# Rebuilding the opening of a fused attention and FFN kernel: 1 KB loads, two-bank score tiles, mixing per head pair, an FFN that begins per k-tile

## The chip, the cores and the metric

The kernel runs on one core of one Trainium2 chip. The metric is the device time in microseconds (us) of one execution. Each execution also has a span (first to last instruction of its trace) and a mean granted TensorE clock; in nearly every run here the time is the span plus 1.7 us.

Executions are compared when they are of the same state: "fast" within 1.5% of the fastest of the same kernel, "slow" above that. A ratio is the mean time of one kernel's fast runs over the mean of the other's in the same rounds, so it is not quite the ratio of the medians quoted beside it. Each call of runs shares one chip and its own runs of the kernel before.

Names: PE is TensorE's matmuls, PEld its weight loads, DVE is VectorE, ACT ScalarE, POOL GpSimd, SP SyncE. L442 is line 442 of the kernel profiled; the same statement has another line number in another kernel.

## The reference, cut to what matters

```python
# 8 batches, 8 heads, 576 positions, head size 64; float32 in and out
scores = q @ k.T / 8 + min(bias, 0), causal mask        # bias from a cumulative sum of s
x = softmax(scores) @ v                                 # heads joined: (8, 576, 512)
u = x + (x.T @ U @ V).T                                 # low rank mixing over positions, rank 32
out = u + relu(u @ w_ch1) @ w_ch2                       # FFN 512 -> 2048 -> 512
```

The FFN is most of the work. It runs in nine groups of 512 rows over the flattened batches. Group 0 lies wholly in batch 0; so no FFN work exists until batch 0 has been through attention and mixing. Everything before that is called the opening here.

## The kernel before: the parts that matter

```python
ps_s = tile_pool(name="ps_s", bufs=4, space=PSUM)   # score tiles, one bank each, 512 columns
ps_w = tile_pool(name="ps_w", bufs=4, space=PSUM)   # everything else
...
# loads, all on one software DMA queue, issued by POOL in this order:
load_qk(0, 0, 2); load_qk(0, 2, 2)       # q and k of batch 0, heads 0-3
...                                      # a memset that the next one waits for
load_qk(0, 4, 4)                         # heads 4-7
load_v(0)                                # v of batch 0: one 256 B row per head and position
U, V, w1, w2
load_qk(1, 0, H); load_v(1)              # batch 1
load(2)                                  # q, k, v of batch 2
...
def spin(n, ps):                         # dummy matmuls that keep TensorE's clock up
...
def scores(n, spins=0):                  # one head pair; 7 exponentials, at most 512 columns
    tail = pscore()
    for hh in range(2):
        diag = pscore()
        ...                              # 4 matmuls
        nc.scalar.activation(pT[:, hh, 0:512], diag, EXP, scale=scale)
        ...                              # mask by a min on DVE
        far = pscore(); ...; mid = pscore(); ...
...
# the opening
for n in range(PB):                      # PB = 4 head pairs of batch 0
    drain(scores(n, 1))
    if n + 2 < PB: drain(transposes(n + 2))
    if n > 0: drain(values(n - 1))
drain(values(PB - 1))
spin(4, pscore)
for _ in seqmix(0):                      # mixing of batch 0, all four pairs together
    spin(2, pscore)
load(2)
fill.append(chanmix(0))                  # FFN of group 0
pace[1] = 8
fill_with(14)                            # 14 of its 16 hidden groups of 4 matmuls
pace[1] = 3                              # from here 3 of 8 calls of step_fill do FFN work
run(transposes(PB))                      # batch 1 begins: needs its q and k
for n in range(PB, NP + 2):              # attention of batches 1-7, FFN steps dealt in between
    ...                                  # pace[1] becomes 7 once batch 1 is mixed
```

In the traces PE runs its matmuls in the program's order. When one stands (sits idle) for a load, the FFN steps behind it are held back, too.

The softmax here doesn't subtract the row's maximum and nothing guards it: scores larger than these inputs give would overflow.

Of the kernel before, what the change touches and what calls it, by code (L numbers as in the profile page):

```python
# [39 lines left out]
def kernel(  # L40
# [12 lines left out]
    nc = tc.nc  # L53
# [21 lines left out]
    ps_s = ctx.enter_context(tc.tile_pool(name="ps_s", bufs=4, space=bass.MemoryType.PSUM))  # L75
    ps_w = ctx.enter_context(tc.tile_pool(name="ps_w", bufs=4, space=bass.MemoryType.PSUM))

    def pscore():
        return ps_s.tile([128, 512], FP32, tag="s", name="pscore")
# [9 lines left out]
    nc.sync.dma_start(out=s_sb, in_=s.rearrange("b h s -> (b h) s"))  # L89

# [6 lines left out]
    def load_qk(b, h, n):  # L97
# [5 lines left out]

    alloc_qk(0)
# [3 lines left out]
    load_qk(0, 2, 2)  # L108

    keep = consts.tile([128, 1, 128], BF16)  # L110
    nc.gpsimd.memset(keep, 3.0e38)
    nc.gpsimd.affine_select(
        out=keep,
        in_=keep,
        compare_op=ALU.is_ge,
        fill=0.0,
        base=0,
        pattern=[[0, 1], [1, 128]],
        channel_multiplier=-1,
    )  # L120


    PW = 1664
    pTs = [consts.tile([128, 2, PW], BF16, name=f"pT{i}") for i in range(2)]

    def ones(ap):
        nc.vector.memset(ap.bitcast(mybir.dt.uint32), 0x3F803F80)

    busy = consts.tile([128, 512], BF16)
    ones(busy)  # L130
# [17 lines left out]
    def spin(n, ps):  # L148
        for _ in range(n):
            dst = ps()  # L150
            nc.tensor.matmul(  # L151
                dst, lhsT=busy[:, 0:128], rhs=busy[:, 0 : dst.shape[1]], start=True, stop=True
            )
# [17 lines left out]
    for dst in (q_t[0], k_t[0]):  # L171
        nc.vector.memset(dst[:, 4:8, 0:2], 0.0)
    load_qk(0, 4, 4)
    init_v(nc.vector, v_slots[0])
    for pT in pTs:
        nc.vector.memset(pT[:, :, 1600:], 1.0)
    U_sb = consts.tile([128, 5, R], BF16)
    nc.vector.memset(U_sb[64:, 4, :], 0.0)

    V_sb = consts.tile([128, 4, S], BF16)  # L180
    nc.vector.memset(V_sb, 0.0)
# [6 lines left out]
    def load_v(b):  # L188
        vt = v_slots[b % 3]
        if 0 < b < 3:  # L190
            init_v(nc.gpsimd, vt)
        for t in range(4):
            nc.gpsimd.dma_start(  # L193
                out=vt[:, t, :, 0:D],
                in_=v[b, :, ds(t * 128, 128), :].rearrange("h p d -> p h d"),
            )
        nc.gpsimd.dma_start(
            out=vt[:64, 4, :, 0:D], in_=v[b, :, 512:576, :].rearrange("h p d -> p h d")
        )

    load_v(0)
    w1_sb = consts.tile([128, 4, FF], BF16)
    w2_sb = consts.tile([128, NF, DM], BF16)
    nc.gpsimd.dma_start(
        out=U_sb[:, :4, :], in_=moe_U[:512].rearrange("(kt kp) r -> kp kt r", kp=128)
    )
    nc.gpsimd.dma_start(out=U_sb[:64, 4, :], in_=moe_U[512:576])
    nc.gpsimd.dma_start(out=V_sb[:R, 0, :], in_=moe_V)
    nc.gpsimd.dma_start(out=w1_sb, in_=moe_w_ch1.rearrange("(kt kp) n -> kp kt n", kp=128))
# [3 lines left out]
    load_v(1)  # L213
# [8 lines left out]


    def transposes(n):
        b, hp = divmod(n, PB)
        slot = slots[n % NSLOT]
        if b > 0:
            nc.sync.dma_start(
                out=slot[D:KA, :, 0 : 2 * S],
                in_=rows_hbm[:, ds(2 * n, 2)].rearrange("r n c s -> r n (c s)"),  # L230
            )
        for hh in range(2):
            h = 2 * hp + hh
            tp = pwork().bitcast(BF16)[:, : 2 * 4 * TP].rearrange(
                "p (c t m) -> p c t m", c=2, t=4
            )
            for c, src in enumerate((q_t[b], k_t[b])):
                for t2 in range(4):
                    nc.tensor.transpose(  # L239
                        tp[:, c, t2, :], src[:, h, ds(t2 * 128, 128)], identity[:TP, :TP]  # L240
                    )
            dst = slot[0:D, hh, 0 : 2 * S].rearrange("p (c m t two) -> p c m t two", c=2, t=4, two=2)
            for par in range(2):
                copy = nc.scalar.copy if n == 0 or (b == 1 and par) else nc.vector.tensor_copy
                copy(  # L245
                    dst[:, :, :, :, par],
                    tp[par * D : par * D + D].rearrange("p c t m -> p c m t"),
                )
            yield

    def scores(n, spins=0):
        slot = slots[n % NSLOT]
        pT = pTs[n % 2]
        tail = pscore()
        for hh in range(2):
            qT = slot[0:KA, hh, 0:S]
            kT = slot[0:KA, hh, S:]

            def mm(dst, j, lo, hi):
                nc.tensor.matmul(  # L260
                    dst,
                    lhsT=kT[:, ds(j * 128, 128)],
                    rhs=qT[:, lo:hi],
                    start=True,
                    stop=True,
                )

            diag = pscore()
            for j in range(4):
                mm(diag[:, ds(j * 128, 128)], j, j * 128, j * 128 + 128)  # L270
            nc.scalar.activation(pT[:, hh, 0:512], diag, EXP, scale=scale)  # L271
            nc.vector.tensor_tensor(  # L272
                pT[:, hh, 0:512].rearrange("p (a b) -> p a b", a=4),
                pT[:, hh, 0:512].rearrange("p (a b) -> p a b", a=4),
                keep.to_broadcast([128, 4, 128]),
                op=ALU.min,
            )
            mm(tail[:, ds(hh * 64, 64)], 4, 512, S)
            spin(spins, lambda: tail[:, 128:512])
            yield  # L280
            far = pscore()
            mm(far[:, 0:448], 0, 128, S)
            mm(far[:, 448:512], 3, 512, S)
            nc.scalar.activation(pT[:, hh, 512:1024], far, EXP, scale=scale)  # L284
            mid = pscore()
            mm(mid[:, 0:320], 1, 256, S)
            mm(mid[:, 320:512], 2, 384, S)
            nc.scalar.activation(pT[:, hh, 1024:1536], mid, EXP, scale=scale)
            spin(spins if hh == 0 else 0, lambda: tail[:, 128:512])
            if hh == 1:  # L290
                nc.scalar.activation(
                    pT[:, :, 1536:1600],
                    tail[:, 0:128].rearrange("p (a b) -> p a b", a=2),
                    EXP,
                    scale=scale,
                )
                nc.vector.tensor_tensor(  # L297
                    pT[:, :, 1536:1600],
                    pT[:, :, 1536:1600],
                    keep[:, :, 0:64].to_broadcast([128, 2, 64]),  # L300
                    op=ALU.min,
                )
            yield
# [7 lines left out]
    def values(n):  # L311
# [5 lines left out]
        x_sb, pT, vt = x_of[b], pTs[n % 2], v_slots[b % 3]  # L317
# [29 lines left out]
    def seqmix(b):  # L347
        x_sb = x_of.pop(b)
        up = pwork()[:, 0:128]
        for dt in range(4):  # L350
            for t in range(5):
                nc.tensor.matmul(  # L352
                    up[:, ds(dt * R, R)],
                    lhsT=x_sb[:, dt, t, :],
                    rhs=U_sb[:, t, :],
                    start=(t == 0),
                    stop=(t == 4),
                    skip_group_check=True,
                )
# [69 lines left out]

    out_flat = out.rearrange("b s d -> (b s) d")  # L430

    def chanmix(g):
        hT = work.tile([128, NF, 512], BF16, tag="hT", name="hT")
        u = uT_of.pop(g)
        u_sd = work.tile([128, 4, 4, 128], BF16, tag="u_sd", name="u_sd")
        nc.sync.dma_start_transpose(
            out=u_sd.rearrange("p a b c -> p (a b) c"), in_=u.rearrange("p a b -> p (a b)")
        )
        for nf in range(NF):
            f1 = pwork()  # L440
            for kt in range(4):
                nc.tensor.matmul(  # L442
                    f1,
                    lhsT=w1_sb[:, kt, ds(nf * 128, 128)],
                    rhs=u[:, kt, :],
                    start=(kt == 0),
                    stop=(kt == 3),
                )
            nc.scalar.activation(hT[:, nf, :], f1, RELU)  # L449
            yield  # L450
        for i in range(4):
            f2 = pwork()
            for nf in range(NF):
# [5 lines left out]
                    stop=(nf == NF - 1),  # L459
# [4 lines left out]
            nc.vector.tensor_tensor(  # L464
                o_sb.rearrange("p (a b) -> p a b", a=4),
                f2.rearrange("p (a b) -> p a b", a=4),
                u_sd[:, :, i, :],
                op=ALU.add,
            )
# [30 lines left out]
    spin(9, pscore)  # L500
    for n, spins in ((0, (2, 6)), (1, (2, 4))):
        for hh, _ in enumerate(transposes(n)):
            spin(spins[hh], pscore)
    for n in range(PB):
        drain(scores(n, 1))
        if n + 2 < PB:
            drain(transposes(n + 2))
        if n > 0:
            drain(values(n - 1))
    for dt in range(1, 4):  # L510
        nc.vector.tensor_copy(V_sb[ds(dt * R, R), dt, :], V_sb[:R, 0, :])
    drain(values(PB - 1))
    spin(4, pscore)
    for _ in seqmix(0):
        spin(2, pscore)
    in_program_order(tc, traced, [E.DVE, E.Activation, E.SP])

# [7 lines left out]
    fill.append(chanmix(0))  # L525
    pace[1] = 8
    fill_with(14)
    pace[1] = 3
    run(transposes(PB))
    for n in range(PB, NP + 2):  # L530
# [5 lines left out]
        if n < NP:  # L536
            run(scores(n))
# [3 lines left out]
        if PB < n <= NP:  # L541
            run(values(n - 1))
# [39 lines left out]
```

## Time and profile before

| | |
|---|---|
| time, median of 3 | 400.19 us (399.95 to 400.25) |
| span of the profiled execution | 403.4 us, mean clock 0.970 |
| PE busy | 382.8 us (95%) |
| dummy matmuls (L151) | 53, 23.7 us of record time |
| first FFN matmul | 44.0 us |
| k of batch 1 landed, first used | 55.4 us, 56.2 us |

These are lines of the page's second part: the busy share of PE, the granted clock and the DMA engines' busy share in tenths, in 40 slices of 10 us.

```profile
PE   7798998798999999999999999999999999999995
...
PEclk9758999999999999999999999999999999999999
DMA  5999999999399359837992599251224014301002
```

After the first 100 us PE is full and its clock whole. All of the time to win lies in the first ten slices. There the clock falls to 0.5, and DMA is full until 100 us.

The view of windows says how busy each engine was in a stretch; the last three numbers are the granted clock, the DMA share and the GB/s moved.

```profile
core 0: us, PE busy (x) PEld busy (x) DVE busy (x) ACT busy (x) POOL busy (x), PEclk, DMA share, GB/s
14.00:31.00 17.00, 15.41 (x153) 11.98 (x152) 11.81 (x25) 10.06 (x21) 9.54 (x14) 0.51 1.53 202
36.00:42.00 6.00, 4.97 (x29) 2.60 (x30) 2.21 (x6) 0.58 (x1) 0.00 (x0) 0.72 1.25 206
50.00:63.00 13.00, 11.41 (x89) 6.05 (x87) 3.40 (x5) 10.25 (x18) 3.40 (x6) 1.00 2.04 93
76.00:84.00 8.00, 6.09 (x50) 3.24 (x47) 5.37 (x10) 2.14 (x5) 2.94 (x4) 0.79 2.24 138
```

And PE's timeline around 76 us (start, duration, what, idle time before it and what ended that):

```profile
76.00 0.30 PE L239 MATMUL pwork<-identity,q_sd 72*128 72x72 bf16 x4
78.20 0.30 PE L239 MATMUL pwork<-identity,k_sd 72*128 72x72 bf16 x4 [1.91 <-DMA k_sd<-in_k_dram]
78.33 0.29 PE L239 MATMUL pwork<-identity,q_sd 72*128 72x72 bf16 x4
78.47 0.29 PE L239 MATMUL pwork<-identity,k_sd 72*128 72x72 bf16 x4
78.59 1.38 PE L454 MATMUL pwork<-w_sb,hT 128*128 128x512 bf16 x4
79.77 0.68 PE L260 MATMUL pscore<-slot_94 68*128 68x128 bf16 x5
80.27 1.90 PE L454 MATMUL pwork<-w_sb,hT 128*128 128x512 bf16 x4
```

PE stood 1.91 us for k of batch 2, and after it four FFN matmuls took 1.90 us instead of 1.03: the clock had been halved. The list of PE's waits (who waited for what, total us, times, longest) begins so:

```profile
PE pwork L239 <- DMA k_sd<-in_k_dram: 4.2, 4, 1.9
PE pwork L352 <- DVE x_sb L333: 2.6, 2, 1.6
```

### The profile page before, as it was taken

Reading aid. Unit: us, or ns where it says so; the run is one execution under the profiler, and the core shown is the slowest. Engines: PE = TensorE matmul, PEld = TensorE weight load, DVE = VectorE, ACT = ScalarE, POOL = GpSimd, SP = SyncE. Lnnn points to the kernel's source line nnn. Section 1 sums busy time; section 2 is a strip of 40 time slices with the busy share of each in tenths; the row PEclk is TensorE's granted clock in tenths of the full one; section 3 lists DMA queues with packets and bytes.
Section 4 is the critical chain, followed back from the end, with each engine's and each line's share of the span. In section 5 each row is a group of like instructions: output and inputs, shape, how many; then the busy total and the mean of one; then the engine's idle time right before and its main releaser. Section 6 shows DMA issues by size and latency. Waiting matters only on the chain.

```text
span 403.4 us, 8541 instructions
## 1 busy us (share of the span) xinstructions
PE 382.8 (95%) x3525; PEld 218.2 (54%) x3525; DVE 223.3 (55%) x484; ACT 201.0 (50%) x384; POOL 56.3 (14%) x79
## 2 busy tenths in 40 slices
PE   7798998798999999999999999999999999999995
PEld 3575445465555556655555565555565554444442
DVE  7875124587756775667566856785678353002011
ACT  5552479551874358534853386328642930530710
POOL 5750023320230041003200230000000000000000
PEclk9758999999999999999999999999999999999999
DMA  5999999999399359837992599251224014301002
GB/s 76 169 211 207 151 93 102 134 151 105 61 153 111 73 97 137 79 72 112 147 80 72 100 151 70 63 122 21 19 70 120 18 34 130 80 18 69 19 26 79
DMA packets 94149, 38.33 MB, mean 95 GB/s; under 512 B 77150, under 2 KB 88446, under 8 KB 94110
## 3 DMA queue, kind: packets, MB, share of 16 engines
q0 software_dynamic: 53360, 18.44, 59.8%
q1 hardware_dynamic: 40750, 19.35, 26.7%
q8 instruction: 27, 0.44, 0.5%
q14 instruction: 12, 0.10, 0.1%
HBM read 37.51 MB, written 9.95 MB: 118 GB/s over the span
## 4 chain that ended last, share of the span: by engine, by line
PE 82%; DMA 10%; DVE 5%; POOL 1%; issue 1%; ACT 1%; DVEq 0%; ACTq 0%
PE pwork L454 29%; PE pwork L442 29%; PE pscore L260 10%; DMA k_sd<-in_k_dram 7%; PE pwork L323 6%; PE pwork L239 3%; DMA v_slot_102<-in_v_dram 2%; DVE o_sb L464 1%; PE pscore L151 1%; PE pwork L395 1%; DVE x_sb L333 1%; PE pwork L352 1%; DMA hT<-in_s_dram 1%; POOL v_slot_102 L193 1%; ACT pT_87 L271 0%
## 5 line engine op out<-in xcount | busy, mean ns | idle before, releaser
L454 PE MATMUL pwork<-w_sb,hT 128*128 128x512 bf16 x576 | 142.2, 381 | 0.2 <-ACT slot_96 L245 0.2
L442 PE MATMUL pwork<-uT,w_sb 128*128 128x512 bf16 x576 | 141.0, 379 | 0.6 <-ACT slot_96 L245 0.3
L449 ACT ACTIVATE hT<-pwork 128x512 bf16<-128x512 f32 x144 | 87.8, 609 | 107.7 <-PE pwork L442 107.1
L454 PEld LDWEIGHTS <-hT 128*128 128x128 bf16 x576 | 51.8, 98 | 49.1 <-issue 0.8
L442 PEld LDWEIGHTS <-w_sb 128*128 128x128 bf16 x576 | 50.6, 98 | 47.4 <-DVE uT L377 0.7
L464 DVE TENSOR_TENSOR o_sb<-pwork,u_sd 128x512 f32<-128x512 f32 x36 | 24.9, 692 | 63.8 <-PE pwork L454 62.6
L271 ACT ACTIVATE pT_87<-pscore 128x512 bf16<-128x512 f32 x32 | 19.3, 603 | 30.7 <-PE pscore L260 30.6
L333 DVE TENSOR_TENSOR x_sb<-pwork,rec 128x320 bf16<-128x320 f32 x64 | 31.3, 490 | 2.0
L271 ACT ACTIVATE pT_86<-pscore 128x512 bf16<-128x512 f32 x32 | 19.3, 603 | 19.5 <-PE pscore L260 19.4
L99 POOL DMA_DIRECT2D q_sd<-in_q_dram x10 | 8.1, 811 | 142.1 <-PE pwork L239 126.6
L245 DVE COPY slot_96<-pwork 64x576 bf16<-64x576 bf16 x22 | 17.4, 797 | 13.9 <-PE pwork L239 13.6
L272 DVE TENSOR_TENSOR pT_87<-pT_87,keep 128x512 bf16<-128x512 bf16 x32 | 13.2, 416 | 20.5 <-ACT pT_87 L271 20.5
L272 DVE TENSOR_TENSOR pT_86<-pT_86,keep 128x512 bf16<-128x512 bf16 x32 | 13.2, 414 | 18.5 <-ACT pT_86 L271 18.4
L239 PEld LDWEIGHTS <-q_sd 72*128 72x128 bf16 x256 | 16.3, 100 | 13.2 <-DMA q_sd<-in_q_dram 1.3
L239 PE MATMUL pwork<-identity,k_sd 72*128 72x72 bf16 x256 | 19.2, 201 | 4.2 <-DMA k_sd<-in_k_dram 4.2
L377 DVE TENSOR_TENSOR uT<-pwork,xT 128x256 bf16<-128x256 f32 (+6 forms) x54 | 19.4, 418 | 6.4 <-PE pwork L395 6.4
L323 PEld LDWEIGHTS <-pT_86 128*128 128x128 bf16 x480 | 19.0, 100 | 7.2 <-issue 2.0
L332 DVE RECIPROCAL rec<-pwork 128x5 f32<-128x5 f32 x64 | 12.2, 192 | 19.2 <-PE pwork L323 18.9
L284 ACT ACTIVATE pT_87<-pscore 128x512 bf16<-128x512 f32 x32 | 19.5, 610 | 6.2 <-PE pscore L260 6.2
L284 ACT ACTIVATE pT_86<-pscore 128x512 bf16<-128x512 f32 x32 | 19.5, 611 | 4.7 <-PE pscore L260 4.6
L245 DVE COPY slot_93<-pwork 64x576 bf16<-64x576 bf16 x26 | 20.6, 796 | 2.0 <-PE pwork L239 1.6
L323 PEld LDWEIGHTS <-pT_87 128*128 128x128 bf16 x480 | 18.8, 100 | 5.3 <-DVE pT_87 L297 0.3
(100 smaller groups left out, 441.3 us busy)
## 6 DMA issues: line engine op xcount, KB each, us to landing
out_dram<-o_sb SPq DMA_DIRECT2D x36, 256.0 KB
w_sb<-in_moe_w_ch_dram POOLq DMA_DIRECT2D x2, 2048.0 KB, 20.8
q_sd<-in_q_dram POOLq DMA_DIRECT2D x7, 576.0 KB, 8.4
k_sd<-in_k_dram POOLq DMA_DIRECT2D x7, 576.0 KB, 14.0
v_slot_102<-in_v_dram POOLq DMA_DIRECT2D x12, 128.0 KB, 13.5
v_slot_103<-in_v_dram POOLq DMA_DIRECT2D x12, 128.0 KB, 15.3
v_slot_104<-in_v_dram POOLq DMA_DIRECT2D x8, 128.0 KB, 17.6
rows_hbm<-hT SPq DMA_DIRECT2D x1, 504.0 KB
```

Of the source, the lines that this page charges most:

```text
L239: nc.tensor.transpose(tp[:, c, t2, :], src[:, h, ds(t2 * 128, 128)], identity[:TP, :TP])
L245: copy(dst[:, :, :, :, par], tp[par * D : par * D + D].rearrange("p c t m -> p c m t"),)
L260: nc.tensor.matmul(dst, lhsT=kT[:, ds(j * 128, 128)], rhs=qT[:, lo:hi], start=True, stop=True,)
L271: nc.scalar.activation(pT[:, hh, 0:512], diag, EXP, scale=scale)
L272: nc.vector.tensor_tensor(pT[:, hh, 0:512].rearrange("p (a b) -> p a b", a=4), pT[:, hh, 0:512].rearrange("p (a b) -> p a b", a=4), keep.t ...
L284: nc.scalar.activation(pT[:, hh, 512:1024], far, EXP, scale=scale)
L323: nc.tensor.matmul(po[:, i, :], lhsT=pT[:, hh, ds(place(j, i), 128)], rhs=vt[:, j, h, :], start=(j == 0), stop=(j == i), skip_group_check= ...
L333: nc.vector.tensor_tensor(x_sb[:, hp, :, ds(hh * D, D)], po[:, :, 0:D], rec.to_broadcast([128, 5, D]), op=ALU.mult,)
L442: nc.tensor.matmul(f1, lhsT=w1_sb[:, kt, ds(nf * 128, 128)], rhs=u[:, kt, :], start=(kt == 0), stop=(kt == 3),)
L449: nc.scalar.activation(hT[:, nf, :], f1, RELU)
L454: nc.tensor.matmul(f2, lhsT=hT[:, nf, ds(i * 128, 128)], rhs=w2_sb[:, nf, :], start=(nf == 0), stop=(nf == NF - 1),)
L464: nc.vector.tensor_tensor(o_sb.rearrange("p (a b) -> p a b", a=4), f2.rearrange("p (a b) -> p a b", a=4), u_sd[:, :, i, :], op=ALU.add,)
```

## The change

Its intent is to start the FFN earlier. It has these parts:

- **Loads.** q and k of batch 0 are issued in four pieces without the memset between them. v of batch 0 comes in 1 KB rows (four positions of one head) into a scratch tile; matmuls with a 0/1 selection matrix spread them over the partitions. w1 comes in two halves. v of batch 1 is issued only after the opening's masks.
- **Scores.** Two-bank PSUM tiles of 1024 columns (2 buffers for 4), so 4 exponentials per head pair for 7, in every batch. In the opening, POOL masks pairs 1 to 3.
- **Mixing and FFN.** Each head pair of batch 0 is mixed by itself; the first four hidden groups take their k-tiles (128 of the 512 features of u, one head pair's) as they come. 12 hidden groups, not 14, follow before batch 1.
- **Residual of group 0.** 16 identity matmuls into the FFN's accumulator in place of a DMA transpose of u and an addition on DVE.
- Dummy matmuls fall from 53 to 25.

```diff
-    ps_s = ctx.enter_context(tc.tile_pool(name="ps_s", bufs=4, space=bass.MemoryType.PSUM))
+    ps_s = ctx.enter_context(tc.tile_pool(name="ps_s", bufs=2, space=bass.MemoryType.PSUM))
...
     load_qk(0, 2, 2)
+    load_qk(0, 4, 2)
+    load_qk(0, 6, 2)
...
+    nc.gpsimd.dma_start(
+        out=v_raw.rearrange("p h t d -> p h (t d)"),
+        in_=v[0, :, 0:512, :].rearrange("h (p t) d -> p h (t d)", t=4),
+    )
...
-    for dst in (q_t[0], k_t[0]):
-        nc.vector.memset(dst[:, 4:8, 0:2], 0.0)
-    load_qk(0, 4, 4)
...
-    load_v(0)
...
+            near = pscore()
             for j in range(4):
-                mm(diag[:, ds(j * 128, 128)], j, j * 128, j * 128 + 128)
+                mm(near[:, ds(j * 128, 128)], hh, j, j * 128, j * 128 + 128)
+            mm(near[:, 512:960], hh, 0, 128, S)
+            mm(near[:, 960:1024], hh, 3, 512, S)
+            nc.scalar.activation(pT[:, hh, 0:1024], near, EXP, scale=scale)
...
+    def v_tile(j, copy):
+        src, rows_in = (v_raw, 128) if j < 4 else (v_raw_end, 16)
+        pv = pwork()
+        for t in range(4):
+            nc.tensor.matmul(
+                pv.rearrange("p (h d) -> p h d", h=H),
+                lhsT=sel[:rows_in, ds((3 + 128 * j if j < 4 else 3) - t, 128)],
+                rhs=src[:, :, t, :], start=(t == 0), stop=(t == 3),
+            )
+        copy(v_slots[0][:, j, :, 0:D], pv.rearrange("p (h d) -> p h d", h=H))
...
+    drain(values(1, pT_of(1)))
+    step(M0)                              # M0..M3: mixing of pairs 0..3
+    drain(values(2, pT_of(2)))
+    step(M0, M1)
+    drain(values(3, pT_of(3)))
+    step(M1, M2)
...
+    hidden_first(0)
+    step(M2, M3)
+    hidden_first(1)
+    step(M3)
+    hidden_first(2)
+    hidden_first(3)
+    mix_first_end()
...
-    fill.append(chanmix(0))
+    fill.append(chanmix(0, first_hT, 4))
     pace[1] = 8
-    fill_with(14)
+    fill_with(12)
     pace[1] = 3
```

## The prediction

> **What bounds the kernel now.** The busy table has TensorE busy 382.8 of 403.4 us, and stage windows show 39.6 to 39.7 of 40 us from 160 to 320 us: no gain there. The time to win lies before 100 us: 23.7 us of dummy matmuls, a clock of 0.50 from 15 to 31 us, the FFN starting at 44.0 us, and about 6 us of TensorE idle between 56 and 98. Issue and landing times show one load queue served in order: v of batch 0 landed at 22.5, w1 at 33.5, w2 at 44.7, q and k of batch 1 at 50.0 and 55.4 (first used at 55.9), v of batch 1 at 69.5, k of batch 2 at 78.2; for this TensorE stood 1.9 us and then ran at 0.50 clock. The chain of waits follows the same queue ("DMA k" 7%, "DMA v" 2.5%).
>
> **What changes.**
> - v of batch 0 in 1 KB rows, not 256 B. The Trainium skill, "DMA: Bandwidth & Descriptors", section "Why small descriptors are slow (HBM only)", tells of a fixed overhead per packet; the trace agrees (7.0 us for 0.6 MB of v, 10.4 us for 2.1 MB of w1). q and k of batch 0 are issued without the pause that leaves DMA at 0.25 from 7 to 9.5 us. I estimate 5 us together: w1 starts near 18, w2 lands near 39.5, k of batch 1 near 48.5.
> - Group 0's transpose of u, which competes with those loads, goes; 16 identity matmuls (0.9 us) replace it.
> - Spins fall from 53 to 25. Added: 20 selection matmuls, 5 evictions of about 0.7 us, masks on POOL (0.29 us at 128x128, longer at 512).
> - Exponentials of 1024 columns: from 603 ns at 512 and 290 at 128 I estimate 1.03 us, 0.5 us of ACT saved per pair; useful only in batch 1, where ACT is full.
> - Mixing per pair and FFN per k-tile shorten the serial tail (34 to 44 us).
>
> **Critical path.** ACT (four pairs at 3.4 us from about 12), then values and mixing, end the opening at 31 to 36 us; 12 hidden groups of 0.865 us end at 42 to 46. Then batch 1's transposes need k, near 48.5. So the load queue sets the gain, not the rebuilt compute: TensorE stands 2 to 6 us and restarts cold (idle before a 0.50 clock is in this trace). Against 55.9 us: -7.4; two hidden groups moved ahead -1.7; identity matmuls +0.9; cold +1; the stand for k of batch 2 and its cold stretch gone, -3 to -4. Sum: about -11 us.
>
> **Prediction: 388.5 us, range 384 to 394.** Faster by over 2%: 0.80; within 2%: 0.18; slower: 0.02.
>
> **What would show it.** First FFN matmul at 28 to 34 us; w1 landed by 29; k of batch 1 landing at 46 to 51, and TensorE waiting for it at the first batch-1 transposes, its longest wait; no wait above 1 us for k of batch 2; windows after 160 us unchanged; a cold clock in part of 14 to 30.
>
> **What would make it wrong.** If 1 KB rows aren't faster, k comes at 53 and the gain is under 2%. If the opening stays cold, or POOL's masks queue behind its load issues, the opening ends after 37 and is the limit. If two two-bank score buffers stall TensorE in the steady state (the third tile waits for the first exponential), each 0.3 us over 28 pairs costs 8 us. v of batch 1, issued only after POOL's masks, could come late.

## The result, and the profile after

The changed kernel takes 395.88 us (393.75 to 396.60, 4 runs) against 400.22 us (399.95 to 402.61, 4 runs). The ratio is 0.9868, with a 95% interval of 0.9830 to 0.9907: some 1.3% faster, which a threshold of 2% calls the same. The predicted 388.5 us and its range, 384 to 394, are missed.

Yet the profiled spans are 403.4 and 394.9 us, 8.5 apart, where the timed medians are 4.3 apart. And what the prediction said of the trace came about. The same views of the profile after:

```profile
PE   7899698989999899999999999999999999999995
...
PEclk9999969999999999999999999999999999999999
DMA  7999999994995399229932997140224025302002
```

```profile
core 0: us, PE busy (x) PEld busy (x) DVE busy (x) ACT busy (x) POOL busy (x), PEclk, DMA share, GB/s
14.00:31.00 17.00, 16.35 (x246) 11.65 (x244) 14.59 (x34) 12.34 (x17) 10.47 (x18) 1.00 1.18 211
36.00:42.00 6.00, 6.00 (x30) 2.70 (x29) 0.83 (x3) 4.67 (x8) 0.22 (x1) 1.00 1.30 201
50.00:63.00 13.00, 11.62 (x87) 6.47 (x84) 5.82 (x11) 9.64 (x12) 3.93 (x5) 0.74 2.58 116
76.00:84.00 8.00, 7.39 (x131) 5.47 (x129) 7.06 (x18) 3.03 (x4) 0.00 (x0) 1.00 1.95 135
```

```profile
45.41 0.38 PE L533 MATMUL pwork<-uT,w_sb 128*128 128x512 bf16 x1
45.63 0.30 PE L275 MATMUL pwork<-identity,q_sd 72*128 72x72 bf16 x4
49.19 0.30 PE L275 MATMUL pwork<-identity,k_sd 72*128 72x72 bf16 x4 [3.27 <-DMA k_sd<-in_k_dram]
...
51.21 1.87 PE L557 MATMUL pwork<-w_sb,hT 128*128 128x512 bf16 x4 [0.94 <-ACT slot L280]
52.87 1.06 PE L290 MATMUL pscore<-slot 68*128 68x128 bf16 x6
53.74 1.90 PE L557 MATMUL pwork<-w_sb,hT 128*128 128x512 bf16 x4
```

```profile
PE pwork L275 <- DMA k_sd<-in_k_dram: 4.1, 3, 3.3
PE pwork L397 <- DVE uxT L393: 1.9, 4, 0.6
```

The opening now runs at full clock in this execution. PE reaches batch 1 at 45.6 us, ten us sooner than before, and then stands 3.27 us for its k. The stand is where the rebuilt compute meets the load queue. It ends with the clock halved from 50.4 us for 6.83 us. The wait for k of batch 2 is gone, and a new wait has appeared (L397 for uxT, 1.9 us in total, where the corresponding wait before was 0.8).

### The profile page after: what moved, and what is told of

Its sections match the earlier page's. It is cut to its first block, busy times and chain, and to the rows that moved or that the text cites. A ratio compares the mean times of both kernels' runs of the same rounds, so it can differ in the third digit from the quotient of the medians.

```text
span 394.9 us, 8383 instructions
## 1 busy us (share of the span) xinstructions
PE 376.8 (95%) x3532; PEld 213.4 (54%) x3532; DVE 223.0 (56%) x480; ACT 194.5 (49%) x290; POOL 62.3 (16%) x89
## 4 chain that ended last, share of the span: by engine, by line
PE 81%; DMA 10%; DVE 3%; ACT 2%; POOL 2%; issue 1%; DVEq 0%; POOLq 0%
PE pwork L557 31%; PE pwork L533 28%; PE pscore L290 9%; DMA k_sd<-in_k_dram 8%; PE pwork L355 6%; PE pwork L275 3%; DMA hT<-in_v_dram 2%; PE pwork L427 1%; ACT pT L315 1%; DVE o_sb L569 1%; ACT slot L280 1%; POOL q_sd L108 1%; POOL k_sd L108 1%; PE pwork L384 1%; ACT pT L322 0%
## 5 line engine op out<-in xcount | busy, mean ns | idle before, releaser
L533 PE MATMUL pwork<-uT,w_sb 128*128 128x512 bf16 x560 | 136.5, 379 | 0.2
L280 DVE COPY slot<-pwork 64x576 bf16<-64x576 bf16 x114 | 90.6, 798 | 21.3 <-PE pwork L275 18.7
L315 ACT ACTIVATE pT<-pscore 128x1024 bf16<-128x1024 f32 x60 | 61.1, 1026 | 48.4 <-PE pscore L290 48.3
L290 PEld LDWEIGHTS <-slot 68*128 68x128 bf16 x576 | 44.2, 98 | 29.4 <-issue 3.1
L290 PE MATMUL pscore<-slot 68*128 68x128 bf16 (+4 forms) x512 | 57.6, 249 | 1.8 <-ACT pT L315 0.8
L302 DVE TENSOR_TENSOR pT<-pT,keep 128x512 bf16<-128x512 bf16 (+1 forms) x87 | 30.3, 354 | 51.2 <-ACT pT L315 30.2
L355 PEld LDWEIGHTS <-pT 128*128 128x128 bf16 x900 | 33.6, 98 | 10.6 <-DVE uT L409 0.7
L355 PE MATMUL pwork<-v_slot,pT 128*128 128x65 bf16 x900 | 35.8, 194 | 0.9 <-DVE o_sb L569 0.5
L322 ACT ACTIVATE pT<-pscore 128x1024 bf16<-128x1024 f32 x30 | 31.2, 1041 | 3.4 <-PE pscore L290 2.7
L365 DVE TENSOR_TENSOR x_sb<-pwork,rec 128x320 bf16<-128x320 f32 x64 | 31.2, 490 | 1.9
L218 POOL DMA_DIRECT2D v_slot<-in_v_dram x28 | 24.9, 909 | 6.0 <-DMA v_slot<-in_v_dram 3.6
L275 PE MATMUL pwork<-identity,q_sd 72*128 72x72 bf16 x256 | 18.9, 197 | 1.1 <-DMA q_sd<-in_q_dram 0.5
```

The source lines that it names most:

```text
L275: nc.tensor.transpose(tp[:, c, t2, :], src[:, h, ds(t2 * 128, 128)], identity[:TP, :TP])
L280: copies(n, hh, par)(dst[:, :, :, :, par], tp[par * D : par * D + D].rearrange("p c t m -> p c m t"),)
L290: nc.tensor.matmul(dst, lhsT=slot[0:KA, hh, ds(S + j * 128, 128)], rhs=slot[0:KA, hh, lo:hi], start=True, stop=True,)
L302: nc.vector.tensor_tensor(dst, dst, keep[:, :, 0:w].to_broadcast([128, n_tiles, w]), op=ALU.min,)
L315: nc.scalar.activation(pT[:, hh, 0:1024], near, EXP, scale=scale)
L322: nc.scalar.activation(pT[:, :, 1024:1536], mid.rearrange("p (a b) -> p a b", a=2), EXP, scale=scale)
```

## The experiments

Fourteen runs. All gave correct results. The first four shared a chip, then four, four and two.

### The two kernels again: `before_again`, `after_again`, `before_look`

No edit. If the profile that the prediction stood on was not typical, a second one would show it.

> The kernel before, unchanged, profiled a second time. The first profile of it spans 403.4 us while its timed runs are 400.2 us; the changed kernel's timed runs are 1.7 us above their spans (395.9 against 394.1). Theory A (the profile that the prediction was built on is a slow execution of the kernel before): this profile spans about 398.5 us, some 4 to 5 us less than the first, and the difference lies before 100 us (a shorter wait for k of batch 2, or a shorter stretch at half clock). Theory B (the two kernels differ in what lies outside the span): spans near 403 again. Ratio 1.000.

Measured: 400.73 us (398.85 to 407.78, 6 runs), ratio 1.0004. The profiled execution was slow once more: span 406.1 us at a mean clock of 0.966.

> The changed kernel, unchanged, a second profile. Both theories: 394 to 396 us timed, ratio 0.985 to 0.990; span 392 to 395; a wait of TensorE of 2 to 4 us for k of batch 1 near 46 us, and half clock for 5 to 7 us after it.

Measured: 395.68 us (394.01 to 397.68), ratio 0.9889 (0.9855 to 0.9922), span 393.9 us. The wait for k of batch 1 was 3.1 us, the half clock 6.83 us from 48.2.

> A third profile of the kernel before. Over 17 runs of it the span goes with the clock: 397.0 to 398.0 us where the mean clock is 0.983 (about 13.5 us at half clock), 399 to 400 at 0.976 (19 us), 406 to 407 at 0.966 to 0.969; the profile behind the prediction had 24 us and 403.4 us. If that profile was only an unlucky one, this one has about 13 to 20 us at half clock and 397 to 401 us, in a stretch of the opening or after the wait for k of batch 2 that is shorter. If the profiler itself slows this kernel, it is again over 403.

Measured: 399.54 us, span 397.8 us. This third execution is like most of the timed ones. (The clock is not all of it, though: two of the runs at a mean clock of 0.983 that the expectation counts spanned 398.9 and 399.0 us.) Its windows and waits, to be laid beside those of before:

```profile
core 0: us, PE busy (x) PEld busy (x) DVE busy (x) ACT busy (x) POOL busy (x), PEclk, DMA share, GB/s
14.00:31.00 17.00, 14.50 (x157) 11.35 (x155) 12.09 (x27) 10.07 (x22) 9.68 (x14) 0.60 1.48 202
36.00:42.00 6.00, 5.16 (x48) 2.96 (x49) 2.79 (x8) 1.17 (x2) 0.00 (x0) 1.00 1.25 205
50.00:63.00 13.00, 11.31 (x103) 6.38 (x102) 4.40 (x7) 10.93 (x19) 5.83 (x9) 1.00 2.28 129
76.00:84.00 8.00, 7.70 (x93) 4.92 (x92) 7.81 (x16) 5.01 (x10) 1.56 (x2) 1.00 2.35 117
```

```profile
PE pwork L352 <- DVE x_sb L333: 2.6, 2, 1.6
PE pwork L239 <- DMA k_sd<-in_k_dram: 1.7, 2, 1.2
```

And its timeline at the place where before stood at 76 us:

```profile
73.78 0.29 PE L239 MATMUL pwork<-identity,q_sd 72*128 72x72 bf16 x4
73.91 0.29 PE L239 MATMUL pwork<-identity,k_sd 72*128 72x72 bf16 x4
...
74.56 1.03 PE L454 MATMUL pwork<-w_sb,hT 128*128 128x512 bf16 x4
```

Three things differ. The half clock near 38 us is absent (1.00 for 0.72). Between 50 and 63 us all DMA together moved 129 GB/s for 93; of this the load queue had 1.26 MB for 0.72 (`--dma`), and nearly all the rest was the DMA transpose of group 0's u, which ran beside it until 56 us here and until 63 in the slow profile. And the stand for k of batch 2 with its cold stretch is absent (1.00 for 0.79 from 76 to 84 us). Read from the traces, in us:

| | before, slow profile | before, usual (`before_look`) | after | after again |
|---|---|---|---|---|
| first FFN matmul | 44.0 | 42.2 | 30.4 | 30.7 |
| k of batch 1 lands | 55.4 | 53.6 | 49.1 | 49.3 |
| PE begins on it | 56.2 | 54.4 | 49.2 | 49.3 |
| k of batch 2 lands | 78.2 | 70.5 | 63.3 | 64.7 |
| first FFN matmul of group 1 | 98.3 | 92.7 | 88.4 | 87.4 |
| from there to the end | 305.1 | 305.1 | 306.5 | 306.5 |
| span | 403.4 | 397.8 | 394.9 | 393.9 |

So against the usual execution the change gains 3 to 4 us of span, as timed; 5.6 us of the 8.5 in the first pair of profiles are the difference between two executions of the same kernel. Over all 55 timed runs of the kernel before 15 took over 402 us, and 5 of them over 405.

### One part alone: `loads_only`

```diff
 # on the kernel before
+    load_qk(0, 4, 2); load_qk(0, 6, 2)            # no memset between
+    ... v of batch 0 in 1 KB rows, v_tile(0..4) before the first values
-    load_v(0)
+    ... w1 in two halves
```

> The kernel before with only the new loads of batch 0 (q and k in pieces of two heads without the pause, v in 1 KB rows with its 20 selection matmuls and 5 evictions, w1 in halves); scores, mixing and the start of the FFN as before. If the opening's compute (FFN from 44.0 us, at half clock for 17 us) is a second limit just behind the queue: k of batch 1 lands at 49 to 52, TensorE gets there only at 56 to 60, and the time stays within 2 us of before, since only the stand for k of batch 2 is gained. If the queue alone was the limit, this gets most of the gain: 396 us.

Measured: 402.04 us (400.31 to 404.19), ratio 1.0029 (0.9989 to 1.0070). k of batch 1 landed at 48.9 us, as early as in the changed kernel, but PE began on it only at 58.7, since its own opening (first FFN matmul at 46.5) had grown by the selection matmuls: PE was at them from 18.3 to 26.6 us, 1.9 us of it waiting for their copies, and at half clock from 23.4. The clock does not hide a gain: two of the six runs had 1.00, and spanned 398.6 and 399.1 us. The loads alone win nothing.

### The change without the 1 KB rows: `small_rows`

```diff
 # on the changed kernel
-    ... v of batch 0 in 1 KB rows, selection matrix, v_tile(0..4)
+    load_v(0)                                     # 256 B rows, straight into place
```

> The changed kernel with v of batch 0 loaded as before, in 256 B rows straight into place, no selection matmuls. If the rows matter through the load queue: w1 starts 2 to 4 us later, k of batch 1 lands at 51.5 to 53 instead of 49.2, TensorE (with 4.3 us less to do) stands 8 to 10 us for it, and the time rises by 2 to 4 us against the changed kernel (398 to 400). Rival: the selection matmuls and their evictions cost as much as the rows save; then the same within 1 us.

Measured: 399.32 us (397.38 to 400.47), ratio 0.9945 (0.9906 to 0.9984). k landed at 53.3, and PE, there at 48.2 us, stood for it:

```profile
48.24 0.30 PE L258 MATMUL pwork<-identity,q_sd 72*128 72x72 bf16 x4
53.37 0.42 PE L258 MATMUL pwork<-identity,k_sd 72*128 72x72 bf16 x4 [4.83 <-DMA k_sd<-in_k_dram]
```

The stand was shorter than expected because this opening lost its clock for 13.65 us. By the ratios the time is 2.2 to 3.1 us above the changed kernel's, as expected; how much of that is the clock and how much the rows is not separated. So about half of the gain needs the rows and the rebuilt compute together: the loads alone gave 0.3% the wrong way, which is within the noise, and the rest (with the other new loads still in) 0.6%. In the kernel before, PE and the load queue reach batch 1 within 0.8 us of each other, and shortening either leaves the other.

### Does the stand cost its cold clock? `warm_stand`

```diff
     fill_with(12)
+    spin_some(16)                                 # 3.5 us of dummy matmuls
     pace[1] = 3
```

> The changed kernel with 16 dummy matmuls (3.5 us at full clock) put where TensorE stands for k of batch 1, just before the first batch-1 transposes. If the load queue decides when batch 1 begins and the stand costs a cold clock (half clock from 50.9 to 57.3 us: three groups of four FFN matmuls at 1.7 instead of 0.86 us and two score groups, about 3 us lost), then k lands as before at about 49 us, the dummies cost nothing, the clock stays 1.00, and the time falls by 2 to 3.5 us against the changed kernel. If TensorE's own work sets the pace, the time rises by up to 3.5 us.

Measured: 395.37 us (394.60 to 397.85), ratio 0.9889 (0.9852 to 0.9926), beside 0.9889 of the changed kernel on the same chip. 3.5 us more work for PE cost nothing, so PE does not set the start of batch 1. From k's first use to group 1 the profile has 36.5 us (49.9 to 86.4) for 38.1 and 39.2 in the two profiles of the changed kernel: the warm clock is worth 1.6 to 2.7 us there. But the median hardly fell: in three of six runs the clock was 1.00 and the span 392.9 us, in the other three it was 0.990 to 0.995 and the span 394.2 to 396.1. The profiled one lost its clock at 130.9 us, at the mixing of batch 2.

### Do the two-bank tiles cost the steady state? `steady_one_bank`

```diff
     # the opening as changed; then its PSUM pool is closed and one of four one-bank tiles opened
-            run(scores(n, pT_of(n)))
+            run(scores_one_bank(n, pT_of(n)))     # the kernel before's scores
```

> The changed kernel's opening with the old one-bank score tiles from batch 1 on. The first pair of profiles shows the changed kernel ahead by 9.9 us when the FFN of group 1 starts but only by 8.2 to 8.5 us at the end. If the two-bank tiles cost that in the steady state, this is 1 to 2 us faster than the changed kernel (ratio to before about 0.983). If they are neutral there: the same within 0.5 us. If they help (fewer, longer exponentials while ACT is full in batch 1): 0.5 to 1.5 us slower.

Measured: 396.28 us (395.69 to 399.20), ratio 0.9907 (0.9870 to 0.9945). From group 1 to the end 306.1 us for 306.5. The tiles are not what the late stretch lost; the small difference of the times is within their spread.

### What costs 1.4 us after group 1 begins? `pace_shift`

```diff
     fill_with(12)
+    pace[0] += 2                                  # count as if 14 steps had been dealt
     pace[1] = 3
```

> The changed kernel with the counter that deals out FFN steps moved on by 2 (it counts 12 instead of 14 steps before batch 1 in the changed kernel; every eighth call is left without FFN work). From the first FFN matmul of group 1 to the end the kernel before took 305.1 us in all three of its profiles and the changed kernel 306.5 in both; in the changed kernel TensorE waits 1.5 us for uxT and 0.8 for ux after that point, in the kernel before 0.4 and 0.4. If the left-out steps fall on the serial steps of the mixing, the shift brings that stretch to 305.1 to 305.5 us and the uxT waits to 0.4; the time falls by 0.5 to 1.4 us. If the two-bank score tiles cost it, nothing changes.

Measured: 394.98 us (392.55 to 395.60), ratio 0.9838 (0.9804 to 0.9872). From group 1 to the end 305.4 us. PE's waits in that stretch, first of the changed kernel, then of this one:

```profile
PE pwork L397 <- DVE uxT L393: 1.5, 3, 0.6
PE pwork L427 <- DVE ux L399: 0.8, 2, 0.4
```

```profile
PE pwork L397 <- DVE uxT L393: 0.6, 1, 0.6
PE pwork L427 <- DVE ux L399: 0.4, 1, 0.4
```

Every eighth call of the filler does no FFN work. With 12 steps for 14 the count is shifted, and the empty calls fell on the mixing's serial steps (matmul, copy on DVE, matmul), in which PE has nothing else to do. Moving the count back recovers 1.1 of the 1.4 us in the trace. (The expectation's "all three" is one too many: `before_again` took 306.6 us there, with a half clock at 143.9 us.)

### Does group 0's transpose compete with the loads? `u_by_dma`

```diff
 # on the changed kernel, group 0 too:
+        nc.sync.dma_start_transpose(out=u_sd..., in_=u...)
-        ... 16 identity matmuls, copy to o_sb
+        nc.vector.tensor_tensor(o_sb, f2, u_sd, op=ALU.add)
```

> The changed kernel with the residual of group 0 by a DMA transpose of u, as before, and no identity matmuls in its FFN. The prediction said that this transpose competes with the loads: then k of batch 1 lands at 51 to 53 instead of 49.2, TensorE stands 2 to 4 us longer, and the time rises by 1 to 3 us. Rival: the transposes run beside the loads without delaying them; then the time falls by up to 0.9 us, the identity matmuls.

Measured: 398.83 us (396.84 to 402.46), ratio 0.9950 (0.9902 to 0.9997). k landed at 51.2 us. Against the changed kernel's 0.9868 and 0.9889, that is 2.4 to 3.3 us. The transpose does take from the load queue: while its packets ran, from 42 to 52 us, the queue moved 0.73 MB, against 1.25 and 1.33 in the two profiles of the changed kernel. But not all of the time is the queue. In the profiled execution the opening, too, had 6.83 us of half clock, PE came to batch 1 only at 49.0 us, and 1.6 us were lost after group 1 began (308.1 us, with a half clock at 134.4). k itself was 0.9 to 2.1 us later than in the six profiles with the changed kernel's loads and no transpose (49.1 to 50.3).

### Does the interleaving pay? `serial_mix`

```diff
     drain(values(1, pT_of(1)))
-    step(M0)
     drain(values(2, pT_of(2)))
-    step(M0, M1)
     drain(values(3, pT_of(3)))
+    step(M0); step(M0, M1)
     step(M1, M2)
...
+    step(M2, M3); step(M3); mix_first_end()
+    for kt in range(4): hidden_first(kt)          # all hidden work after all mixing
```

> The changed kernel with the mixing of all four head pairs only after the last values, and the first four hidden groups only after the mixing: the interleaving taken out. If the load queue sets when batch 1 begins, the opening's end moves 1 to 3 us later but TensorE only stands that much less for k of batch 1 at 49 us, and the time is the same within 0.7 us. If the interleaving pays, the time rises by 1 to 3 us.

Measured: 396.99 us (394.43 to 398.02), ratio 0.9883 (0.9844 to 0.9922), beside 0.9868 and 0.9889 of the changed kernel. PE came to batch 1 at 48.0 us instead of 45.6, and still stood 2.1 us for k (landed at 50.3). The mixing per head pair and the FFN per k-tile, as such, are off the critical path.

### A better order of the loads: `k_first`, `k_first_warm`

```diff
 # k_first, on the changed kernel
-    nc.gpsimd.dma_start(out=w2_sb, ...)
     alloc_qk(1)
     load_qk(1, 0, H)
+    ... w2 in two halves
 # k_first_warm: that, and
+    pace[0] += 2
-    for n, spins in ((0, (2, 4)), (1, (3, 3))):
+    for n, spins in ((0, (2, 6)), (1, (4, 4))):
     ... 2 and 4 for 1 and 1 dummy matmuls around the first scores
```

> The changed kernel with q and k of batch 1 loaded before w2, and w2 in two halves. If the load queue's order is what TensorE stands for at 46 us: k of batch 1 lands near 40, the stand of about 3.3 us and the half clock after it go, w2 lands near 45 and 50, and the time falls by 3 to 6 us against the changed kernel, to about 391 us (ratio to before 0.975). Rival: the stand only moves, to w2's second half near 50 us or to v of batch 1 near 58 us; then the gain is under 1.5 us.

Measured: 394.80 us (392.08 to 395.74), ratio 0.9837 (0.9799 to 0.9875). k landed at 39.6, and w2's halves at 44.2 and 49.7. But in the profiled execution the opening ran at half clock from 15.4 us for 6.83, and PE reached batch 1 at 49.4 us, with nothing to stand for: the stand had hidden that loss in the changed kernel, and here it counts. One of six runs had a clock of 0.998, and a span of 390.4 us.

> k of batch 1 before w2, the counter moved on by 2, and 8 more dummy matmuls in the stands between 7 and 16 us. k_first had two kinds of runs: 390.4 us of span at mean clock 0.998, and 392.5 to 394.0 with 7 to 8 us at half clock, in its profile from 15.4 us on. If the clock of the opening is what is left once k comes early, most runs are near 1.00 and the median falls to about 391 us timed (ratio 0.976). Rival: the stands after 50 us (w2's second half, v of batch 1) take it back, then 393 or more.

Measured: 391.41 us (390.38 to 392.24, 6 runs), ratio 0.9754 (0.9723 to 0.9786): 2.5% faster than the kernel before, where the change as given was 1.1 to 1.3%. All six runs had clocks of 0.996 to 1.000. PE's timeline at the start of batch 1:

```profile
45.92 0.29 PE L279 MATMUL pwork<-identity,q_sd 72*128 72x72 bf16 x4
46.05 0.29 PE L279 MATMUL pwork<-identity,k_sd 72*128 72x72 bf16 x4
...
49.44 1.02 PE L561 MATMUL pwork<-w_sb,hT 128*128 128x512 bf16 x4 [0.58 <-DMA w_sb<-in_moe_w_ch_dram]
```

No stand at 46 us; 0.58 us is left for w2's second half. It beats both kernels. Three edits are in it, and their shares are not separated: in this profile the moved count shows no gain (306.8 us from group 1 to the end, with a half clock at 127.9 us).

### What makes the kernel before slow in some executions? `before_warm`, `before_ident`

```diff
 # before_warm: more dummy matmuls in the opening's stands
-    drain(scores(n, 1))
+    drain(scores(n, 5 if n == 0 else 1))
+    ... 6 before the third transposes, 4 more in those of pair 1, 10 for 4 before the mixing
 # before_ident: the residual of group 0 by identity matmuls, as in the change
```

> The kernel before with dummy matmuls in the stands of its opening (between 11 and 16 us and before the mixing at 34 us), nothing else. If the extra time of its slow executions begins with the half clock of the opening (44.0 instead of 42.2 us at the first FFN matmul in the two slow profiles, which have a half-clock stretch near 38 us that the fast one lacks), then the first FFN matmul comes at 36 to 41 us, the runs at 400 us and above vanish, and the median falls by 1 to 3 us. Since k of batch 1 lands at 53 to 55 us, it can't fall by more. Rival: slow executions come from the load queue alone, whatever the clock: then runs over 402 us remain and the median stays within 0.7 us.

Measured: 400.49 us (399.29 to 401.10, 6 runs), ratio 0.9985 (0.9951 to 1.0020). Of the opening's half clock 6.83 us were left (from 23.1 us). The first FFN matmul came at 41.9 us, not at 36 to 41, so the opening before was not bound by its clock alone: v of batch 0 landed at 22.6 us, as there (22.5). No run was over 402 us, but with 15 of 55 over it in the unchanged kernel, six runs without one can be chance (an estimate: (40/55)^6, or 0.15).

> The kernel before with the residual of group 0 by 16 identity matmuls instead of the DMA transpose of u, nothing else. In the slow profiles of before [...] the transposes ran until 63 instead of 56 us. If the transposes' place beside the loads of k and v of batch 1 makes the slow executions: k lands at 50 to 52, v of batch 1 by 60, TensorE never stands for k of batch 2, no run is over 402 us, and the median falls by 0.5 to 2 us (TensorE itself reaches batch 1 only at 54 to 56). Rival: no effect but the identity matmuls' 0.9 us: slower by 0.5 to 1.

Measured: 400.27 us (399.43 to 403.28), ratio 0.9985 (0.9946 to 1.0025). k landed at 53.8 and not at 50 to 52; v of batch 1 at 61.8 and k of batch 2 at 66.7 us for 62.5 and 70.5. One run of six took 403.28 us, so the transpose is not needed for an execution over 402. Without it the load queue moved 1.66 MB between 50 and 63 us, against 1.26 in the usual execution and 0.72 and 0.69 in the two slow ones; fast runs gained nothing from that. What makes the slow executions, the clock or the load queue's rate, stays open.

## Why the prediction was wrong

**What held.** The mechanism did, to within a microsecond or two:

| predicted | measured |
|---|---|
| first FFN matmul at 28 to 34 us | 30.4, 30.7 |
| hidden groups end at 42 to 46 | 45.8 (record of the last), 46.1 |
| k of batch 1 near 48.5 | 49.1, 49.3 |
| PE stands 2 to 6 us for it, its longest wait | 3.3, 3.1 |
| 1024-column exponential 1.03 us (estimate) | 1026 ns, mean of 60 |
| no wait above 1 us for k of batch 2 | none |
| two-bank tiles might stall PE | they do not (`steady_one_bank`) |

The load queue does set the gain (`warm_stand`, `serial_mix`), and the rows and the transpose do act through it (`small_rows`, `u_by_dma`). Misses without consequence: w1 was whole at 31.2 us, not by 29, but its first half, at 24.5, is all that the early FFN needs; and the opening was not cold in this profile, though in others of its relatives it was.

**The step that failed is the base of the sum.** The prediction took "Against 55.9 us: -7.4" and "the stand for k of batch 2 and its cold stretch gone, -3 to -4" from a profile that spans 403.4 us, and subtracted the sum, "about -11 us", from a timed median of 400.2 us. With 1.7 us between span and time, the timed runs span about 398.5, and `before_look` spans 397.8. In that usual execution PE begins on batch 1 at 54.4 us, 1.8 earlier, mostly because the half clock near 38 us is absent (in neither did PE wait for k there: it had landed 0.8 us before); and from there to group 1 it takes 38.3 us instead of 42.1, 3.8 less, because there is no stand for k of batch 2 and no cold stretch after it. These two are the 5.6 us between the two profiles of before (group 1 at 98.3 and at 92.7). The change could not gain them from runs most of which never lost them.

In the sum, term by term, between the usual execution and the changed kernel's profiles:

| term | predicted | measured |
|---|---|---|
| start of batch 1 | -7.4 | -5.2 (54.4 to 49.2), -5.1 |
| hidden groups, identity matmuls, cold restart, stand for k of batch 2 | -2.8 to -3.8 | +0.9, -0.2 (38.3 to 39.2, 38.1) |
| group 1 to the end | 0 | +1.4 (305.1 to 306.5) |
| total | about -11 | -2.9, -3.9 of span; -4.3 timed |

**Two smaller terms.** "Cold +1" was low: the half clock lasted 6.83 us, and `warm_stand` puts it at 1.6 to 2.7. "Windows after 160 us unchanged" is true of their busy shares (39.5 to 39.7 of 40), and yet the stretch from group 1 on grew by 1.4 us, because two steps fewer in the opening moved the filler's empty calls onto the mixing; `pace_shift` recovers 1.1 of it.

Against the profile that it was built on, the prediction was off by about 2 us (394.9 and 393.9 measured, 403.4 less "about 11" expected). The range was too narrow because it held only the uncertainty of the change, not that of the base.

**What stays open.** Why the kernel before has slow executions. Both slow profiles have a half clock near 38 us that the usual one lacks. In both the transpose of group 0's u is issued 1.9 us later (43.7 for 41.9 us) and runs beside the loads for 14 us instead of 10, and the load queue moves little over half as much from 50 to 63 us (0.72 and 0.69 for 1.26 MB). That the one leads to the other is not shown: neither experiment settled it. Nor is a low clock needed in every case: three of the 15 timed runs over 402 us had a mean clock of 0.979, 0.979 and 0.982, and the usual profile had 0.980.

## What to carry to other kernels

Before pricing a change from a profile, lay the profile's span beside the timed runs: a span above the timed median belongs to another execution, and its waits may not be in the runs that you will be compared with. Where the engine and the load queue arrive at a point within a microsecond of each other, a part of a change that shortens one of them may win little or nothing alone; ask what the other will still wait for, and reorder the loads by first use (here k of batch 1 before w2, with more dummy matmuls and a shifted count, doubled the gain). When a schedule deals work by a counter, changing the number of steps in one place moves its gaps everywhere later.

## What the Trainium skill lacked or had wrong

- "TensorE: Matmul & The Clock Gate", section "Part 1: The HAM clock gate": the window of about 3.4 us agrees (half clock came in 3.41, 6.83, 13.65 and 17.07 us, which is 1, 2, 4 and 5 windows). The page gives an idle window, or gaps over about 3.4 us, as what halves the clock, and tells further down of a kernel in which short idle times between groups did it; it has no figure for how much idle time in a window is enough. Here, in the 3.41 us before the half clock, PE had been busy 1.51 us (before, 79.1 us; the stand was 1.91), 1.77 (38.2 us) and 2.06 us (`warm_stand`, 130.9 us, where the longest wait was 0.64): windows 40 to 56% idle. But busy time alone does not decide: `before_look` and `before_ident` had a window with the same 1.77 us and kept the clock (34.1 and 34.4 us on, counted in steps of 3.41 us from the clock's own changes).
- The same section puts the ramp's penalty under 1% of a typical span and advises against fitting it. That is said of the ramp, not of a half clock that comes back, as it did here several times: from run to run the kernel before had 13.5 to 27.6 us of it (worked out as 2 x (1 - mean clock) x span), and spans of 397.1 to 399.0 us at a mean clock of 0.983, 398.9 to 401.1 at 0.976, 405.7 to 407.0 at 0.966 to 0.970 (but also 401.9 and 402.3 at 0.979).
- "DMA: Bandwidth & Descriptors", section "Why small descriptors are slow (HBM only)": the direction agrees, v of batch 0 in 1 KB rows brought k of batch 1 in 3.0 to 4.2 us earlier (49.1 to 50.3 us in the six profiles with the changed kernel's loads, 53.3 with small rows). The prediction's 7.0 us for v is no clean figure: in them another queue moved 0.5 MB (`rows_hbm`), too.
- No page has a figure for what a DMA transpose takes from a load queue beside it: from 42 to 52 us that queue moved 0.73 MB with a transpose (`u_by_dma`) and 1.25 and 1.33 MB without (the changed kernel).
- No page has the time of a mask (affine select) on POOL: 0.63 to 0.65 us for 128x512 bf16, 0.30 for 128x128.
